# First keys loaded as soon as there is a place, the last weight blocks rounded in place, and two blocks moved out of the first layer

## The chip, the cores and the metric

One core of a Trainium2 chip. The metric is device time in microseconds (us) of one execution. All runs quoted are in the fast state. Line numbers (L871) are those of each kernel's own source, so one statement has several: the first layer's ReLU is L871 before and L874 after the change.

## The reference

An attention block feeds a Fourier mixing block with a two-layer network. Eight batches, 576 rows, 8 heads of 64:

```python
q_s = softmax(q, axis=-1);  k_s = softmax(k, axis=2)      # q, k, v: (8, 8, 576, 64)
kv = np.einsum('bhsd,bhse->bhde', k_s, v)
x = np.einsum('bhsd,bhde->bhse', q_s, kv)                 # then to (8, 576, 512)
mixed = np.real(np.fft.fft(np.fft.fft(x, axis=1), axis=2))
u = x + mixed
un = (u - mean(u)) / np.sqrt(var(u) + 1e-06)
out = u + np.maximum(un @ w_ch1, 0.0) @ w_ch2             # w_ch1: 512x2048, w_ch2: 2048x512
```

(Shortened: the two softmax lines stand for maximum, exp, sum and division; the casts are left out.)

## The kernel before

The rows are worked in groups. The first group runs both layers as plain products while the weights are still being made: 32 blocks of 64-bit words are loaded (16 for each layer), and each is rounded to the form that the products read. Later groups use combined weights made from these, stored and loaded again. While a group's products run on TensorE, the other engines prepare the attention and the spectrum of the next one: the *folds* are sums and differences of rows and columns, most of them on VectorE (tile `eo`), then TensorE multiplies them with the Fourier table, and ScalarE copies that spectrum out of PSUM (tiles `Z` and `ZT`). Tiles of this kernel lie in SBUF, the working memory, or in PSUM, where all its products go; "acc", "ba", "bb" and "bc" are PSUM buffers (banks).

A block is rounded by three engines. ScalarE scales the high half into PSUM (line 343 of the whole text), VectorE shifts and merges it from there (L344, L345), ScalarE scales the low half (L348), and GpSimd adds the two (L349):

```python
def convert(i):
    pair = raws.pop(i).rearrange("p (n w) -> p n w", w=2)
    lo, hi = pair[:, :, 0], pair[:, :, 1]
    # ... out: the block's place in w1sb or w2sb
    n = ("bc", "bb", "bc", "bb")[i] if i < 4 else "acc"
    t = self.ps.tile([P, 512], F32, tag=n, name=n, bufs=3 if i >= 4 else 1)[:]
    to = self.halves()[:, 0:D] if i == NF else out
    ti, V = t.bitcast(I32), nc.vector
    nc.scalar.activation(t, hi.bitcast(F32), ACT.Copy, scale=2.0 ** -112)
    V.tensor_scalar(out=to.bitcast(I32), in0=ti, scalar1=3, scalar2=None, op0=ALU.logical_shift_left)
    V.scalar_tensor_tensor(out=to.bitcast(I32), in0=ti, scalar=-(1 << 31), in1=to.bitcast(I32),
                           op0=ALU.bitwise_and, op1=ALU.bitwise_or)
    nc.scalar.activation(lo, lo.bitcast(U32), ACT.Copy, scale=2.0 ** -29)
    nc.gpsimd.tensor_tensor(out=out.bitcast(I32), in0=to.bitcast(I32), in1=lo, op=ALU.add)
```

Words share places in SBUF. This table says which; the load of block 29 takes the place of block 25, that of block 31 the place of block 26, and each is issued when the sum of the older block is done:

```python
WORDS_AT = [*range(8), 8, 9, 10, *range(3, 8), 0, 1, 2, 8, 9, 10, 4, 5, 6, 7, 8, 11, 12, 7, 13, 8]
```

The first layer ends each of its 16 columns with a ReLU on ScalarE, from one of three PSUM banks; between the columns blocks are rounded, and the rest go between the down products:

```python
for f in range(NF):
    up[f]()          # 4 x 128 rows of products into "ba", "bb" or "bc", then the ReLU on ScalarE
    free(f)
    round_blocks(range(4 + n * f // NF, 4 + n * (f + 1) // NF))      # n = 2 * NF - 14
rest = [lambda i=i: round_blocks([i]) for i in range(4 + n, 2 * NF)]
# ... later, among the down products:
for step in rest[i // 3:i // 3 + 1] if i % 3 == 0 else []:
    step()
```

The keys of a batch's first two blocks, at the end of the folds (`t` is a result of the last fold):

```python
for r in range(2):
    k, v = self.key_places()
    self.nc.vector.tensor_copy(k[0:1, 0:1], t[0:1, 0:1])         # L518, L519: hold the load back
    self.nc.vector.tensor_copy(v[0:1, 0, 0:1], t[0:1, 0:1])
    self.keys_to(b, r, k, v)
```

## Time and profile before

| | before |
|---|---|
| median of 3 runs | 1136.15 us (1133.37 to 1136.38) |
| TensorE busy | 1093.8 of 1135.1 us |
| first group's two layers, first product to the second group's first product | 63.60 to 197.31: 133.7 us |
| the next six groups, to the eighth group's first product | 197.31 to 932.48: 735.17 us |

The two stretches in the last rows are what the change touches, and the document keeps to them. The prediction below reads most of the profile; two more views of the kernel before are needed later. The first is ScalarE's timeline around the first layer's only gap (columns: start us, duration us, engine, line, operation, output and input, count; in brackets the idle time before it and what ended it).

```profile
108.17 0.66 ACT L348 ACTIVATE big<-big 128x512 int32<-128x512 uint32 x1 [6.13 <-DMA big<-in_w_dram]
108.73 0.58 ACT L871 ACTIVATE big<-bb 128x512 f32<-128x512 f32 x1
111.85 0.67 ACT L348 ACTIVATE words<-words 128x512 int32<-128x512 uint32 x1 [2.53 <-DMA words<-in_w_dram]
112.42 0.58 ACT L871 ACTIVATE big<-bc 128x512 f32<-128x512 f32 x1
```

ScalarE's instructions run in the order listed. The low half of block 29 (L348, "big") waits 6.13 us for its words, the ReLU of bank "bb" stands behind it, then the low half of block 31 ("words") waits again, with the next ReLU behind it. So each of the two waits stands before a ReLU, but before a different one, and TensorE has a bank's work in between: it idles 0.98 us.

The second is the queue that issues the loads, SP, with the two loads concerned:

```profile
104.60 0.33 SPq L328 DMA_DIRECT2D big<-in_w_dram  x1
105.84 0.33 SPq L328 DMA_DIRECT2D words<-in_w_dram  x1
```

The words of block 29 are asked for at 104.60 and used from 108.17, 3.57 us later.

### The profile page before, as it was taken

To read this page: it belongs to the slowest core of one execution; us is meant where nothing else is said; L and a number is where in the kernel's file an instruction comes from. 1 tells how busy PE (TensorE), PEld (TensorE's weight loads), DVE (VectorE), ACT (ScalarE), POOL (GpSimd) and SP (SyncE) were. 2 spreads that over 40 slices of the span, in tenths; PEclk is the share of its full clock that TensorE was granted. 3 is DMA by queue.
4 is the path that set the end of the run, shared out by engine and by line. 5 is a ranking of instruction groups with operands and counts; after the bars stand their busy time and mean duration, and the time that the engine had idled before them with its cause. 6 is when DMAs were issued, how large, how long until landed. Compare 5 with 4: busy or idle time off the path is not lost.

```text
span 1135.1 us, 14610 instructions
## 1 busy us (share of the span) xinstructions
PE 1093.8 (96%) x5440; PEld 913.8 (81%) x5440; DVE 543.5 (48%) x1117; ACT 404.0 (36%) x975; POOL 333.7 (29%) x300
## 2 busy tenths in 40 slices
PE   5799989999999999999999999999999999999997
PEld 4644446888888888898889888888889888888886
DVE  6684785477334733484434633583434352203201
ACT  6695614264324423361325232532334152201200
POOL 2065570244022500433023402260034203302320
PEclk9999999999999999999999999999999999999999
DMA  9566686444464344554454535435453344444451
GB/s 308 172 206 212 222 304 201 152 164 167 145 194 161 141 172 145 197 185 151 146 178 150 193 120 196 167 112 183 144 193 149 114 161 152 180 145 155 151 186 55
DMA packets 92582, 193.79 MB, mean 171 GB/s; under 512 B 23121, under 2 KB 59729, under 8 KB 85345
## 3 DMA queue, kind: packets, MB, share of 16 engines
q1 hardware_dynamic: 90712, 191.82, 49.4%
q10 hardware_dynamic: 1800, 1.05, 0.3%
q8 instruction: 43, 0.70, 0.3%
q14 instruction: 27, 0.21, 0.1%
HBM read 168.72 MB, written 28.31 MB: 174 GB/s over the span
## 4 chain that ended last, share of the span: by engine, by line
PE 73%; DVE 10%; DMA 6%; ACT 5%; issue 3%; POOL 2%; SPq 1%; ACTq 0%; POOLq 0%; DVEq 0%
PE bb L939 14%; PE bb L977 12%; PE ba L939 9%; PE bc L939 9%; PE ba L977 7%; PE bc L977 7%; PE acc L560 3%; DMA k<-in_kT_dram 3%; PE acc L642 2%; PE acc L759 2%; DVE eo L681 1%; PE bc L878 1%; PE tr L839 1%; PE tr L546 1%; PE acc L735 1%
## 5 line engine op out<-in xcount | busy, mean ns | idle before, releaser
L939 PE MATMUL bb<-unT,big 128*128 128x256 f32 x768 | 187.4, 381 | 0.8 <-DVE u L911 0.8
L977 PE MATMUL bb<-big 128*128 128x256 f32 x768 | 172.4, 379 | 4.5 <-DVE u L907 4.5
L977 PEld LDWEIGHTS bb<-big 128*128 128x128 f32 x768 | 145.1, 190 | 25.8 <-DVE u L907 5.7
L939 PEld LDWEIGHTS bb<-unT,big 128*128 128x128 f32 x768 | 142.8, 190 | 24.6 <-DVE u L907 2.6
L355 POOL TENSOR_TENSOR big<-big 128x512 f32<-128x512 f32 (+1 forms) x38 | 46.6, 1226 | 307.6 <-ACT big L951 306.8
L939 PE MATMUL bc<-unT,big 128*128 128x256 f32 x512 | 125.3, 379 | 0.0
L951 ACT ACTIVATE big<-big 128x512 f32<-128x512 f32 x96 | 60.3, 629 | 179.0 <-DVE big L950 178.5
L939 PE MATMUL ba<-unT,big 128*128 128x256 f32 x512 | 123.6, 379 | 0.2 <-ACT unT L843 0.2
L977 PE MATMUL bc<-big 128*128 128x256 f32 x512 | 116.0, 379 | 0.5 <-DVE x L994 0.5
L977 PE MATMUL ba<-big 128*128 128x256 f32 x512 | 114.8, 379 | 0.0
L977 PEld LDWEIGHTS bc<-big 128*128 128x128 f32 x512 | 96.1, 190 | 14.3 <-DVE x L994 0.9
L977 PEld LDWEIGHTS ba<-big 128*128 128x128 f32 x512 | 95.7, 190 | 12.1
L939 PEld LDWEIGHTS bc<-unT,big 128*128 128x128 f32 x512 | 95.1, 190 | 12.6
L939 PEld LDWEIGHTS ba<-unT,big 128*128 128x128 f32 x512 | 95.1, 190 | 12.2 <-ACT unT L843 0.5
L911 DVE TENSOR_TENSOR u<-bb,s 128x512 f32<-128x512 f32 x40 | 27.6, 691 | 144.8 <-PE bb L977 88.2
L599 ACT ACTIVATE q<-q,qm 128x64 f32<-128x64 f32 x240 | 62.1, 339 | 25.1 <-DVE qm L597 25.1
L363 POOL TENSOR_TENSOR unT<-unT 128x512 f32<-128x512 f32 x8 | 14.2, 1772 | 188.7 <-DVE unT L362 188.7
L907 DVE TENSOR_TENSOR u<-bb,s 128x512 f32<-128x512 f32 x40 | 27.6, 690 | 72.2 <-PE bb L939 38.7
L989 POOL TENSOR_TENSOR x<-x,u 128x512 f32<-128x512 f32 x14 | 17.7, 1267 | 143.0 <-DVE u L911 74.6
L950 DVE TENSOR_TENSOR big<-bc,u 128x512 f32<-128x512 f32 x64 | 44.1, 689 | 22.8 <-PE bc L939 21.9
L903 ACT COPY s<-ba 128x512 f32<-128x512 f32 x40 | 23.4, 585 | 85.5 <-PE ba L939 46.2
L843 ACT COPY unT<-tr 128x512 f32<-128x512 f32 x36 | 20.7, 586 | 79.4 <-PE tr L839 78.8
(237 smaller groups left out, 1650.0 us busy)
## 6 DMA issues: line engine op xcount, KB each, us to landing
big<-w1s SPq DMA_DIRECT2D x64, 896.0 KB
big<-w2s SPq DMA_DIRECT2D x56, 1024.0 KB
big<-in_w_dram SPq DMA_DIRECT2D x21, 512.0 KB
q<-in_q_dram SPq DMA_DIRECT2D x27, 256.0 KB
k<-in_kT_dram SPq DMA_DIRECT2D x24, 288.0 KB
v<-in_v_dram SPq DMA_DIRECT2D x24, 256.0 KB
words<-in_w_dram SPq DMA_DIRECT2D x8, 512.0 KB
mirror<-x SPq DMA_DIRECT2D x14, 256.0 KB
```

The costliest lines, as they stand in the source:

```text
L355: e1.tensor_tensor(out=to(4), in0=at(2), in1=at(3), op=ALU.add)
L560: nc.tensor.matmul(pk, lhsT=ks[:, c, :], rhs=v[:, c, :], start=(c == 0), stop=(c == NC - 1))
L599: nc.scalar.activation(heads[:, h, :], heads[:, h, :], ACT.Exp, bias=m[:, h:h + 1])
L642: nc.tensor.matmul(px[:, r * P:(r + 1) * P], lhsT=qT[:, r, :], rhs=self.kvr[b % 2][:, r, :], start=True, stop=True)
L759: nc.tensor.matmul(pm[:, at:at + size], lhsT=z(k)[0:rows], rhs=cd[0:rows, at:at + size], start=True, stop=(k != 0))
L903: nc.scalar.copy(temp("s1"), box["ba"][:])
L907: V.tensor_tensor(out=temp("u2"), in0=box["bb"][:], in1=box["s1"][:], op=ALU.add)
L911: V.tensor_tensor(out=temp("u3"), in0=box["bb"][:], in1=box["s1"][:], op=ALU.add)
L939: nc.tensor.matmul(bank()[:, i, :], lhsT=w[:, WA_AT[m], k * P:(k + 1) * P], rhs=unT[:, B_AT[m], k, :], start=first and i == 0 and k == 0, ...
L950: V.tensor_tensor(out=hp(i), in0=bank[:], in1=u[:], op=ALU.add)
L951: nc.scalar.activation(hp(i), hp(i), ACT.Relu)
L977: nc.tensor.matmul(bank()[:, i, :], lhsT=h[p][:, A_AT[m], i * P:(i + 1) * P], rhs=w[:, p, :], start=first and i == 0 and p == 0, stop=p == ...
```

## The change

It touches three places. The keys' loads no longer wait for the folds; only the maxima of the keys do, by a *gate*: a VectorE instruction on one element that reads the last fold's result and rewrites a word of the loaded keys, so that what reads the keys comes after it. In the first group these loads are also held back: `hold` writes one word of each of their places, late in the first layer, and a load has to wait for that (*held places*). Blocks from 20 on no longer take a PSUM buffer: their high half is scaled in place, in SBUF. Two blocks more move from the first layer to the second.

```diff
-        held = {12: [("q", D, 3)] * 3}
+        held = {12: [("q", D, 3)] * 3, 15: [("k", S, 2)] * 2 + [("v", NC * P, 2)] * 2}
...
-            t = self.ps.tile([P, 512], F32, tag=n, name=n, bufs=3 if i >= 4 else 1)[:]
+            if i < 20:
+                t = self.ps.tile([P, 512], F32, tag=n, name=n, bufs=3 if i >= 4 else 1)[:]
+            else:
+                t = hi.bitcast(F32)
...
             k, v = self.key_places()
-            self.nc.vector.tensor_copy(k[0:1, 0:1], t[0:1, 0:1])
-            self.nc.vector.tensor_copy(v[0:1, 0, 0:1], t[0:1, 0:1])
             self.keys_to(b, r, k, v)
+            self.gate(t, k[0:1, 0:1])
...
-            n = 2 * NF - 14
+            n = 2 * NF - 16
+            turn = [2 * i if i < 4 else 3 * i - 4 for i in range(12)]
...
-                for step in rest[i // 3:i // 3 + 1] if i % 3 == 0 else []:
-                    step()
+                if i in turn:
+                    rest[turn.index(i)]()
```

## The prediction

> **What bounds the kernel now.** I read the page first (busy time of each engine), then TensorE's waits, because a gap on the engine that sets the end is the only thing that a change of waits can win back, then the timelines around the largest gaps.
>
> ```profile
> PE 1093.8 (96%) x5440; PEld 913.8 (81%) x5440; DVE 543.5 (48%) x1117; ACT 404.0 (36%) x975; POOL 333.7 (29%) x300
> ```
>
> TensorE is busy 1093.8 of 1135.1 us; all that it idles is 41.3 us. A table of busy time by stretch splits this: 22.1 us fall before 63.6 us (the start, before the first layer), 5.05 us in 63.6 to 197.3 (the first group's two plain layers), 1.43 us in 197.3 to 320 (second group), 6.36 us in 320 to 1031, and 6.3 us after that. The change takes no TensorE work away, so the stretches that it touches hold 5.05 + 1.43 + 6.36 = 12.8 us, or 1.1% of the time. This is the ceiling, and I see no way to a gain over 2% (22.7 us).
>
> TensorE's waits put names to those gaps (us in total, times, longest):
>
> ```profile
> PE acc L560 <- ACT ks L547: 10.6, 10, 3.6
> ...
> PE bb L977 <- DVE u L907: 4.5, 3, 1.9
> PE acc L642 <- DVE big L345: 3.1, 1, 3.1
> ...
> PE bb L869 <- ACT big L871: 1.0, 1, 1.0
> ```
>
> Of the first, 8.8 us lie before 60 us and the other three waits, 0.62 us each, belong to the third key block of a batch, which is not changed. The next three are what the change is about.
>
> **The keys.** The three waits of 4.5 us are at 286, 531 and 777 us, in the second, fourth and sixth group. The last one, on three engines (start, duration, instruction, in brackets the idle time before it and its releaser):
>
> ```profile
> 766.84 0.33 SPq L503 DMA_DIRECT2D k<-in_kT_dram  x1
> 767.27 0.38 SPq L505 DMA_DIRECT2D v<-in_v_dram  x1
> 767.74 0.46 SPq L413 DMA_DIRECT2D big<-w2s  x1
> 768.29 0.38 SPq L503 DMA_DIRECT2D k<-in_kT_dram  x1
> ```
> ```profile
> 766.80 0.13 DVE L518 COPY k<-eo 1x1 f32<-1x1 f32 x1
> ...
> 769.76 0.75 DVE L534 TENSOR_REDUCE km<-k 128x1 f32<-128x576 f32 x1 [2.77 <-DMA k<-in_kT_dram]
> ...
> 776.46 0.75 DVE L534 TENSOR_REDUCE km<-k 128x1 f32<-128x576 f32 x1 [4.66 <-DMA k<-in_kT_dram]
> 777.13 0.68 DVE L907 TENSOR_TENSOR u<-bb,s 128x512 f32<-128x512 f32 x1
> ```
> ```profile
> 777.87 1.99 PE L977 MATMUL bb<-big 128*128 128x256 f32 x8 [1.80 <-DVE u L907]
> ```
>
> The tiny copy at the end of the folds lets the key loads go at 766.8; 0.9 us later a 1 MB weight load follows, and the second key block comes behind it. It lands near 776.4, 8.1 us after its issue. Its maximum stands ahead of L907 on VectorE, L907 must empty the bank "bb", and TensorE waits 1.80 us for that bank.
>
> **The rounding.** In the first group TensorE's largest gap ends at 146.28 us:
>
> ```profile
> 144.73 0.68 DVE L344 TENSOR_SCALAR big<-acc 128x512 int32<-128x512 int32 x1
> 145.44 0.69 DVE L345 SCALAR_TENSOR_TENSOR big<-acc,big 128x512 int32<-128x512 int32 x1
> ```
> ```profile
> 146.28 1.13 PE L642 MATMUL acc<-kvr,qT 128*128 128x128 f32 x8 [3.11 <-DVE big L345]
> ```
>
> A rounded block of the second layer holds one of the three "acc" banks from ScalarE's write until VectorE, busy 9.1 of the 10 us from 140 to 150, has read it twice. The product with the queries needs that bank.
>
> [...] (min/median/max in ns):
>
> ```profile
> L604 DVE TENSOR_TENSOR q<-q,qrec x30: 679/693/1604, 124.0 to 857.0; 128x512 f32<-128x512 f32 x30
> L345 DVE SCALAR_TENSOR_TENSOR big<-acc,big x27: 679/681/693, 67.5 to 153.0; 128x512 int32<-128x512 int32 x27
> ```
>
> Two SBUF inputs take up to 1604 ns beside GpSimd; the rounding with one input in PSUM never more than 693. [...]so L344 may gain by reading SBUF. The nearest measure here is L825 (128x512, SBUF to SBUF, a scaling) at 544 ns against 682 ns for L344.
>
> **Part 1, the keys.** Removed: four 0.13 us copies in each of six batches; added: two gates of about 0.14 us. That is nothing. What counts is when the load goes: its place comes free when the previous batch's last two key blocks have been multiplied (228 to 236 us in the second group, instead of 276), 40 us before the folds end. The DMA share in 230 to 240 us was 0.21, so the 1.2 MB (about 3.5 us at the 350 GB/s seen in the full stretches) have room. The gate then finds its data, both maxima follow the folds at once (1.5 us), L907 starts when its bank is full, and the exps no longer hold ScalarE's copies of the spectrum. Gain: 0.80 + 1.92 + 1.80 = 4.5 us. The third and fifth group have the same 8 us load in the chain that ended last, but TensorE had other work and idled only 0.1 to 0.2 us; little comes from there. I book 4.1.
>
> **Part 2, roundings without PSUM.** ScalarE's 0.64 us stays (the other half, SBUF to SBUF, takes 0.67). Twelve blocks lose their PSUM buffer, and the 3.11 us gap goes. Against it stands VectorE's time. From 120 to 166 us VectorE is the tight engine (9.1, 8.2, 9.1, 8.0 and 8.7 us busy in each 10 us), and five blocks are rounded there. L345 now has two SBUF inputs: at worst +0.6 us each, L344 at best -0.14: some +0.3 on average, 1.5 us for five blocks. TensorE needs the folds at 168.39; the first two are ready at 164.6. Of that slack of 3.8 us, 3.1 are used up if TensorE comes earlier, leaving 0.7. So 1.5 - 0.7 = 0.8 us comes back as a wait: gain 3.1 - 0.8 = 2.3 us. Part 1 is needed for this: in 171.0 to 173.7 ScalarE did the key exps late (0.22 us of wait at 174.29), which would otherwise catch an earlier TensorE. The early keys must also give back what they delay at 120 to 130 us, where DMA share was 0.80: the late words (512 KB each) landed at 128.05 and VectorE took the first only at 131.92, so 3 us of delay is free.
>
> **Part 3, two blocks fewer in the first layer.** Blocks 20 and 21 move behind the first down product. Engine order is not text order here: 27 of the 32 roundings (L344) had run by 103.7 us though blocks 22 to 26 are written in the second layer. So the two blocks hardly move in time. The first layer's one gap (0.98 us at 109.46) comes from a ReLU on ScalarE behind a low half that waited 6.13 us for its words; their load is asked for by block 25, not by 20 or 21. Gain 0.3. The four added copies held to the last ReLU of the layer may cost VectorE a short wait near 123 us; part of that 0.3.
>
> Sum: 4.1 + 2.3 + 0.3 = 6.7 us; 1136.15 - 6.7 = 1129.45, I say 1129.5 us.
>
> **Rivals.** (a) *The wait comes back as a DMA wait.* [...]a key load waiting there for its place (waits on L560 of up to 5.9 us are there already) holds back weight or query loads, and queries were late at 724 us (4.38 us). For: the queries go just after, at 245 us. Against: DMA is 47% busy in these groups and weights are four buffers ahead. It would eat part 1: 1133 to 1136. (b) *VectorE becomes the bound of the first group.* If all five roundings double beside GpSimd (+3.5 us) and the held copies stall it by 2 us, the folds end 5 us later, and TensorE gains nothing or loses 2 us there: 1131.5 to 1134. For: VectorE's load; against: GpSimd idles a quarter of that stretch. (c) *All works, and the new order closes small gaps too:* all of 4.5 + 3.1 + 0.98 + 0.5 (the query wait at 135) + 0.4: 9.5 us, 1126.6. (d) *The start is reordered*, since VectorE's and ScalarE's orders are laid out anew: the 22 us of gaps before 63.6 could move by 2 us either way.
>
> **Range and chances.** From (c) with 2 us luck, 1125, to (a) or (b) at their worse end, 1135.5. The runs before spread by 3 us themselves. Faster by over 2% would need nearly twice the ceiling: 0.01. Slower by over 2% needs a new stall of 23 us, over 3 us in every group: 0.02. Within: 0.97.
>
> **What would show it.** Right: "bb L977 <- DVE u L907" near zero among TensorE's waits; key loads issued at the end of the up products; no DMA wait ahead of the maxima L534; "acc L642 <- DVE big L345" gone; L345 at 0.7 to 1.3 us for twelve blocks; a wait under 1.5 us at the first L735 of the first group; the second group starting near 194 instead of 197.3. Wrong: a DMA wait at the gate, queries or weights waited for, TensorE waiting for the folds by over 3 us in the first group, or a start that ends later than 63.6.

## The result, and the profile after

The changed kernel took 1134.22 us (median of 4 runs, 1133.62 to 1136.19) against 1136.27 us for the kernel before on the same chip. The ratio is 0.9991, 95% interval 0.9971 to 1.0011. Ratios here are the mean time of one kernel's fast runs over that of the other's fast runs of the same rounds, so not quite the ratio of the medians. The predicted gain was 6.7 us. Some 1 to 2 us came, and the interval includes no gain at all.

The stretches show that two large things happened, not none:

| us | before | after | gain |
|---|---|---|---|
| start of the first layer | 63.60 | 63.23 | 0.37 |
| first group's two layers | 133.71 | 141.21 | -7.50 |
| next six groups | 735.17 | 727.20 | 7.97 |
| the rest of the profiled span | 202.6 | 202.8 | -0.1 |

**The six groups** gained more than was booked. This is the busy time of each engine in that stretch (start and end, length, then busy us and instructions of TensorE, its weight loads, VectorE, ScalarE and GpSimd; clock, DMA share and GB/s), before, then after:

```profile
197.31:932.48 735.17, 727.38 (x3871) 642.55 (x3871) 366.29 (x750) 264.80 (x658) 201.94 (x165) 1.00 0.47 160
```
```profile
204.44:931.64 727.20, 725.33 (x3871) 643.16 (x3871) 360.87 (x740) 265.13 (x658) 201.79 (x165) 1.00 0.47 162
```

TensorE's gaps are the length less its busy time: 7.79 us before, 1.87 after, so 5.92 us of the gain are gaps. For the other 2.05 us the same 3871 products count less busy time; I did not look into that. What ended the gaps is on VectorE's timeline of the second group, after the change:

```profile
283.74 1.39 DVE L537 TENSOR_REDUCE km<-k 128x1 f32<-128x576 f32 x2
```

Both maxima run at once, with no wait for data. In the second group the first two key blocks are asked for at 235.68 and 254.04, not at 276.04 and 278.35 as before; the prediction had said 228 to 236 for both.

**The first group** lost it. Three of TensorE's waits after the change (us in total, times, longest):

```profile
PE bb L872 <- ACT big L874: 7.4, 1, 7.4
...
PE tr L613 <- issue: 1.6, 2, 1.1
...
PE acc L738 <- ACT ZT L749: 1.1, 1, 1.1
```

"acc <- DVE big", 3.1 us before, is gone, as predicted, and so is "bb <- DVE u". The first line stands in their place. It is the gap of 0.98 us of before, now 7.41 us, on TensorE's timeline after:

```profile
117.21 5.80 PE L872 MATMUL bb<-unT,big 128*128 128x512 f32 x8 [7.41 <-ACT big L874]
122.84 3.60 PE L872 MATMUL bc<-unT,big 128*128 128x512 f32 x8
```

The eight products after the gap take 5.80 us, the next eight 3.60. The granted clock was 1.00 up to 114.5 us, fell within the gap, was 0.50 from 115.5 to 121.2 us and 1.00 from 122.2 us on. From 117.2 to 123.0 us it was 0.63 on average, against 1.00 in the whole of 100 to 130 us before, where the gap was 0.98 us; 0.50 for about 4.3 of the 5.8 us gives both that 0.63 and the 2.1 us lost (my estimate, from 3.67 us for eight products at 1.00 before). So the long gap cost some 2 us more.

ScalarE's timeline after says why TensorE waited:

```profile
111.53 0.65 ACT L347 ACTIVATE big<-big 128x512 f32<-128x512 f32 x1 [9.82 <-DMA big<-in_w_dram]
112.09 0.66 ACT L352 ACTIVATE big<-big 128x512 int32<-128x512 uint32 x1
115.38 0.65 ACT L347 ACTIVATE words<-words 128x512 f32<-128x512 f32 x1 [2.63 <-DMA words<-in_w_dram]
115.94 0.66 ACT L352 ACTIVATE words<-words 128x512 int32<-128x512 uint32 x1
116.49 0.57 ACT L874 ACTIVATE big<-bb 128x512 f32<-128x512 f32 x1
```

Two things differ from before. Both late blocks, 29 and 31, now stand ahead of the one ReLU of "bb" (**order**). And the words of block 29 came at 111.53 instead of 108.17 (**lateness**). For the second, the SP queue after:

```profile
107.98 0.33 SPq L328 DMA_DIRECT2D big<-in_w_dram  x1
110.04 0.33 SPq L328 DMA_DIRECT2D words<-in_w_dram  x1
```

From issue to use it is 3.55 us, as before (3.57). The load went 3.38 us later, because block 25, whose place it needs, was finished later. GpSimd's sums of blocks 24 and 25, before, then after:

```profile
102.04 2.53 POOL L349 TENSOR_TENSOR big<-big 128x512 int32<-128x512 int32 x2 [1.00 <-ACT big L871]
```
```profile
105.01 2.95 POOL L353 TENSOR_TENSOR big<-big 128x512 int32<-128x512 int32 x2 [1.45 <-DVE big L349]
```

They end at 104.57 before and at 107.96 after. After the change they wait for VectorE, and most of the delay arises there (instances of the shift after the change: min/median/max in ns, first and last start):

```profile
L348 DVE TENSOR_SCALAR big<-acc x15: 678/690/692, 65.9 to 91.2; 128x512 int32<-128x512 int32 x15
L348 DVE TENSOR_SCALAR big<-big x5: 415/1489/1507, 97.0 to 112.3; 128x512 int32<-128x512 int32 x5
L348 DVE TENSOR_SCALAR big<-words x4: 415/968/1509, 94.1 to 116.1; 128x512 int32<-128x512 int32 x4
```

The shift from PSUM took 0.68 to 0.69 us in all 15 of these, also where GpSimd was in an addition (67.66, 71.61 and 83.02: 0.68 each). From SBUF it took 0.41 to 0.43 us alone (0.43 at 112.28 and 116.12, GpSimd idle) but up to 1.51 us (at 105.30, with GpSimd adding from 105.01 to 107.96). The six shifts of blocks 20 to 25 take 6.6 us of VectorE's timeline (pairs at 94.07, 97.04 and 102.35) against 3.95 before: 2.65 us more, next to the 3.39 us that block 25 is late. So the durations show the shift from SBUF faster alone, and slower by up to 1.1 us where GpSimd was in an addition (1.29 us alone); they do not show by what mechanism.

The sum of the first group: the ReLU wait 7.41 - 0.98 = 6.43, the half clock 5.80 - 3.67 = 2.13, the new wait for the spectrum's copies 1.15, and less the PSUM wait, 3.11; that is 6.6 us. Another 1.7 us are eight products at the first layer's start that took 5.37 us at a granted clock of 0.68, and 3.67 before; before, the low clock fell some microseconds earlier (0.50 from 53 to 59 us). Other runs show this either way, so I don't count it to the change. Together 8.3 us, against 7.50 measured. Most of the difference is in TensorE's busy time, which rose by 3.2 us in this stretch and not by 2.1 + 1.7; I did not trace it.

### The profile page after: what moved, and what is told of

It is laid out like the page before. It is cut to its first block, busy times and chain, and to the rows that moved or that the text cites. A ratio compares the mean times of both kernels' runs of the same rounds, so it can differ in the third digit from the quotient of the medians.

```text
span 1134.4 us, 14587 instructions
## 1 busy us (share of the span) xinstructions
PE 1094.5 (96%) x5440; PEld 915.5 (81%) x5440; DVE 542.3 (48%) x1109; ACT 404.3 (36%) x975; POOL 335.3 (30%) x304
## 4 chain that ended last, share of the span: by engine, by line
PE 86%; ACT 4%; DMA 3%; DVE 3%; issue 2%; POOL 1%; ACTq 0%; SPq 0%; POOLq 0%; DVEq 0%
PE bb L942 15%; PE bb L980 15%; PE ba L942 10%; PE bc L980 10%; PE bc L942 10%; PE ba L980 10%; PE acc L563 3%; PE acc L645 2%; PE acc L738 2%; PE acc L741 2%; PE acc L762 2%; PE tr L613 1%; PE tr L842 1%; PE bc L881 1%; PE tr L549 1%
## 5 line engine op out<-in xcount | busy, mean ns | idle before, releaser
L602 ACT ACTIVATE q<-q,qm 128x64 f32<-128x64 f32 x240 | 61.6, 339 | 6.1 <-DVE qm L600 6.0
L953 DVE TENSOR_TENSOR big<-bb,s 128x512 f32<-128x512 f32 x32 | 22.1, 690 | 55.6 <-PE bb L942 55.5
```

Source lines behind the costliest of these rows:

```text
L602: nc.scalar.activation(heads[:, h, :], heads[:, h, :], ACT.Exp, bias=m[:, h:h + 1])
L953: V.tensor_tensor(out=hp(i), in0=bank[:], in1=u[:], op=ALU.add)
```

## The experiments

Times are medians; ratios are to the kernel before, with the 95% interval. My theory ("T" in the expectations) was that the keys gain and the in-place roundings lose it again at the first layer's ReLU. The rivals numbered R there are each described in the expectation that names them.

| run | what it is | us | ratio |
|---|---|---|---|
| e1_keys | the keys alone | 1128.86 | 0.9943 [0.9919, 0.9967] |
| e3_nopsum | in-place roundings alone | 1148.16 | 1.0121 [1.0097, 1.0145] |
| e4_two | two blocks fewer alone | 1135.37 | 1.0003 [0.9992, 1.0015] |
| e2_round | the last two together | 1146.48 | 1.0098 [1.0080, 1.0116] |
| e5_behind | change, blocks 29 and 31 behind the last ReLU | 1134.58 | 0.9994 [0.9979, 1.0009] |
| e6_psum20to26 | change, 20 to 26 in PSUM again | 1127.29 | 0.9931 [0.9916, 0.9946] |
| e12_place20to26 | change, 27 to 31 in PSUM again | 1131.80 | 0.9966 [0.9953, 0.9979] |
| e13_adds_dve | change, sums of 20 to 26 on VectorE | 1127.96 | 0.9915 [0.9886, 0.9944] |
| e7_nogate | keys alone, without the gate | 1132.01 | 0.9972 [0.9956, 0.9988] |
| e8_nohold | keys alone, without the held places | 1128.31 | 0.9934 [0.9915, 0.9952] |
| e9_keys_behind | keys, 29 and 31 behind the last ReLU | 1125.20 | 0.9912 [0.9897, 0.9926] |
| e10_best | e9 with 27 to 31 in place | 1128.08 | 0.9943 [0.9924, 0.9962] |

### The parts alone: e1, e3, e4, e2

e1 has the first and third piece of the diff (held places, keys with the gate) on the kernel before.

> Only the key part of the change (early loads, gate, hold); roundings as before. Theory T (the keys gain, the roundings without PSUM lose it again in the first layer): about 1128 us, 8 us under before; the longest wait of TensorE for a ReLU in the first layer stays near 1.0 us; second group starts near 197 us; groups two to seven last 727 us together instead of 735. Rival R1 (the early key loads crowd the first group's words, and so the loss belongs to the keys): second group starts at 203 us or later and the time is 1133 us or more.

Measured: 1128.86 us, a gain of 0.57%, about 6.5 us. Groups two to seven took 727.80 us, all of the full change's gain; the first layer had no long ReLU wait. The keys are not the loss.

e3 has the in-place piece alone:

```diff
-            t = self.ps.tile([P, 512], F32, tag=n, name=n, bufs=3 if i >= 4 else 1)[:]
+            if i < 20:
+                t = self.ps.tile([P, 512], F32, tag=n, name=n, bufs=3 if i >= 4 else 1)[:]
+            else:
+                t = hi.bitcast(F32)
```

> Only the late roundings without PSUM; blocks of the first layer and keys as before. Theory T: ScalarE's halves of blocks 29 and 31 both stand ahead of a ReLU and wait for their words, so TensorE waits 6 to 8 us for that ReLU and then runs slow for some us; second group starts near 204 us; 1142 to 1144 us. Rival R2 (the loss comes from moving blocks 20 and 21): 1132 to 1135 us, no long wait for a ReLU.

Measured: 1148.16 us, 1.2% slower; worse than expected. The ReLU wait is there with 6.8 us, and a second one with it: 4.7 us for ScalarE's copies of the spectrum at the end of the first group.

e4 has the two pieces with `n` and `turn` alone.

> Only the two blocks fewer in the first layer and the new turn; PSUM and keys as before. Theory T: nothing, 1134 to 1137 us, ReLU wait near 1.0 us, second group starts near 197 us. Rival R2: 1142 us or more.

Measured: 1135.37 us, no difference.

e2 has e3's and e4's pieces together, and the keys as before.

> Both rounding parts (no PSUM from block 20, two blocks fewer), keys as before. If the parts add up: the change's 1134.2 plus the 6 to 8 us that the keys gained, 1140 to 1142 us; ReLU wait of 6 to 8 us; second group starts near 204 us. If the two blocks fewer do nothing beside the in-place rounding either, as they did alone: about 1148 us as with the in-place rounding alone, second group near 209 us.

Measured: 1146.48 us; its second group starts at 207.01. The parts don't add up: e1 gains some 6.5 us and e2 loses some 11, which would make 1140, and the full change took 1134. In e2 the copies of the spectrum are waited for 5.4 us, in the full change 1.1. So the early keys are worth more in company than alone. The likely reason is the one that the prediction gives in its part 2: they take the late exps off ScalarE there. No run tests it apart.

### Order or lateness: e5, e6, e12, e13

e5 removes the order. In the whole change, both blocks are gated behind the last ReLU of the layer:

```diff
             f = i % NF
+            if i in (29, 31):
+                self.gate(self.h0[:, NF - 1, :], pair[0:1, 0:1, :])
             out = (self.w1sb if i < NF else self.w2sb)[:, f, :]
```

> The whole change, and a one-element VectorE gate that holds blocks 29 and 31 behind the last ReLU of the first layer; everything else as in the change. Theory T (the order on ScalarE is the loss): no wait for a ReLU at all, second group starts between 193 and 197 us, 1124 to 1128 us. Rival R3 (the roundings from SBUF cost VectorE and GpSimd so much beside each other that the first group is late anyway): second group starts at 201 us or later, 1131 us or more.

Measured: 1134.58 us, no gain. The wait of 7.4 us for the ReLU is gone, but its time came back as several waits of the second layer and the folds, of which two, in TensorE's waits of e5:

```profile
PE acc L739 <- ACT ZT L750: 3.3, 1, 3.3
PE bc L882 <- POOL s L361: 3.3, 1, 3.3
```

The second is named for GpSimd; the last ReLU before it on ScalarE, at 120.30, stood behind exps of the queries, whose load had been issued at 112.60, after the stores of the late blocks, and landed near 117.3. In e9 that load was issued at 108.40. The issue time is not the whole of it: in e6 the load went at 112.61 too, but its exps began at 115.43. My theory that order alone made the loss fell here, with one reservation: the gate may have a price of its own. e10, below, settles that in part.

e6 gives PSUM back to blocks 20 to 26 only:

```diff
-            if i < 20:
+            if i < 27:
```

> The whole change, but blocks 20 to 26 keep their PSUM buffer and only 27 to 31 are rounded in place. ScalarE's order, read before the run, puts one ReLU behind the high half of block 29 and the next behind block 31, not one behind both. Theory T2 (the loss is the order on ScalarE together with words that come late because VectorE and GpSimd slow each other on blocks 20 to 26 in SBUF): block 29's words are waited for until about 108 us as before, TensorE waits 0.5 to 2 us for a ReLU instead of 7.4, second group starts at 193 to 198 us, 1125 to 1131 us. Rival R4 (any late block in place brings the long wait, whatever blocks 20 to 26 do): wait of 5 us or more, 1133 us or more.

Measured: 1127.29 us. This one condition brings back the whole loss: ReLU wait 0.47 us, second group from 194.44 (the prediction had said 194). On ScalarE's timeline of e6 the ReLU of "bb" stands behind one half of block 29 only (L346, the high half) and ahead of block 31, and the words are there at 106.08, not at 111.53:

```profile
106.08 0.67 ACT L346 ACTIVATE big<-big 128x512 f32<-128x512 f32 x1 [6.66 <-DMA big<-in_w_dram]
106.64 0.57 ACT L873 ACTIVATE big<-bb 128x512 f32<-128x512 f32 x1
107.12 0.68 ACT L351 ACTIVATE big<-big 128x512 int32<-128x512 uint32 x1
```

e12 is the opposite: blocks 20 to 26 in place, 27 to 31 in PSUM (`if i < 20 or i > 26`).

> The counterpart of the run with 20 to 26 in PSUM: the whole change, but only blocks 20 to 26 are rounded in place and 27 to 31 keep PSUM. ScalarE's order, read before the run, has the low halves of blocks 29 and 31 both ahead of one ReLU, as in the change. Theory T2: block 29's words are waited for until about 111 us, TensorE waits 5 to 7 us for the ReLU, second group starts at 201 to 206 us, 1131 to 1137 us. Rival R6 (it is the in-place rounding of 29 and 31 itself): wait under 2 us, second group before 199 us, 1130 us or less.

Measured: 1131.80 us. The ReLU wait is 6.7 us, with eight products at 5.82 us after it, though the blocks ahead of the ReLU, 29 and 31, have their PSUM. Its median is some 2.5 us under the full change's (second group from 199.22), but the intervals of the two ratios overlap, so a cost of blocks 27 to 31 on top of 20 to 26 is not shown. In the profiles, 1.7 of the 5.2 us between the starts of the second group are the low clock at the start of the change's first layer; and e12 has no wait for the spectrum's copies, 1.1 us in the change. The shifts in e12:

```profile
L347 DVE TENSOR_SCALAR big<-big x4: 414/1500/1508, 94.8 to 101.6; 128x512 int32<-128x512 int32 x4
L347 DVE TENSOR_SCALAR big<-words x3: 415/1503/1506, 91.9 to 103.1; 128x512 int32<-128x512 int32 x3
```

e13 takes GpSimd out of the collision: in the whole change the sums of blocks 20 to 26 go to VectorE.

```diff
-            nc.gpsimd.tensor_tensor(out=out.bitcast(I32), in0=to.bitcast(I32), in1=lo, op=ALU.add)
+            adder = nc.vector if 20 <= i < 27 else nc.gpsimd
+            adder.tensor_tensor(out=out.bitcast(I32), in0=to.bitcast(I32), in1=lo, op=ALU.add)
```

> The whole change, except that the last addition of blocks 20 to 26 is done by VectorE instead of GpSimd[...]. Question: why are the late words of blocks 29 and 31 asked for 3.4 and 4.2 us later than before? Theory A (collision): the shift of these blocks out of SBUF takes up to 1.5 us because GpSimd adds at the same time; with no GpSimd addition there every shift of blocks 20 to 26 takes about 0.41 us, though VectorE gets seven additions of some 0.7 to 1.2 us more. The load of block 29 is then asked for some 1 to 3 us earlier than in the change (107.98), TensorE's wait for the ReLU falls from 7.4 to 4 to 6 us, time 1129 to 1133. Theory B (the order alone: without PSUM's pace ScalarE simply has both low halves ahead of the ReLU and the words come when the store queue lets them): shifts may get short, but the load still goes at 107.5 to 109, wait 7 us or more, time 1134 to 1137.

Measured: 1127.96 us, ratio 0.9915 (the kernel before took 1137.97 us on that chip, so the ratio is the better figure), and the result was correct. Every shift from "big" is now short, in e13's instances:

```profile
L347 DVE TENSOR_SCALAR big<-big x5: 414/415/428, 97.6 to 108.3; 128x512 int32<-128x512 int32 x5
L347 DVE TENSOR_SCALAR big<-words x4: 414/421/1503, 93.5 to 111.9; 128x512 int32<-128x512 int32 x4
```

The one long shift, near 94 us, starts at the end of one of GpSimd's sums of earlier blocks; in the change the shift of 1.5 us at 94.07 stands beside the next such sum (93.99 to 95.29). The load of block 29 goes on e13's SP queue 4.08 us earlier than in the change:

```profile
103.90 0.33 SPq L328 DMA_DIRECT2D big<-in_w_dram  x1
105.80 0.33 SPq L328 DMA_DIRECT2D words<-in_w_dram  x1
```

This bears out theory A, the collision, and the effect is larger than expected: the longest ReLU wait is 1.4 us. Two reservations. A sum on VectorE is also shorter, 0.68 us against 1.29 to 1.47 for each on GpSimd, so not all of the 4.08 us need be the collision; the 2.65 us above are the part that the shifts show. And with the sums moved, the order on ScalarE changed too; the ReLU of "bb" now runs at 101.36, ahead of both late blocks. So e13 doesn't separate order from lateness. With order mended and the words still late (e5) nothing was won; with both mended (e6, e13) all of it.

### The gate and the held places: e7, e8

e7 is e1 without the line `self.gate(t, k[0:1, 0:1])`.

> Keys loaded early and held in the first group as in the first experiment, but without the gate that holds their maxima behind the folds. Theory T (what counts is that the loads are early): groups two to seven last 727 to 729 us, 1127 to 1130 us. Rival R5 (the gate is what keeps the maxima and the exps from cutting into the folds): groups two to seven last 731 us or more, 1132 us or more.

Measured: 1132.01 us. The six groups took 732.20 us, between 735.17 (before) and 727.80 (e1), one profile each: the early load without a gate is worth about 3.0 us, and the gate saves another 4.4. In e7 the three waits of 4.5 us that the prediction named are gone too, but in the same three groups (the second, fourth and sixth) TensorE waits 1.70, 0.67 and 2.02 us for something else, 4.4 us in all. Its waits over the whole run, of which these are a part:

```profile
PE tr L608 <- issue: 3.2, 3, 1.7
PE tr L608 <- DVE q L602: 2.7, 2, 2.0
```

The queries' transposes wait for VectorE's division of the queries (L602). So the gate is not only a safeguard against a wait for data; by its place it keeps the key maxima behind the folds, and thereby other work in its turn. Before the change the late loads did that; the gate keeps it, and so is not a gain of its own over the kernel before.

e8 is e1 without the held places in `hold`.

> Keys early and gated, but not held in the first group, so the third batch's first keys are loaded as soon as the queue comes to them. In the trace of the change the held keys were issued only at 166 us, not at 120 to 130 us as predicted, so the hold may bind little. If so: 1127 to 1131 us and the second group starts at 195 to 198 us. If the 1.2 MB come at the start, they crowd the first batch's loads: first layer starts 2 us or more later, 1131 us or more.

Measured: 1128.31 us, the same as e1. The held places did nothing here.

### A version that beats both: e9, e10

e9 is e1 with e5's gate for blocks 29 and 31; PSUM and the split of blocks stay as before.

> Only the key part, roundings in PSUM as before, and the low halves of blocks 29 and 31 held behind the last ReLU of the first layer. Theory T: the ReLU wait of about 1 us goes, but the two blocks then come later to VectorE and hold their PSUM buffers later; second group starts at 195 to 198 us; 1127 to 1131 us, no clear gain over the keys alone. If the order on ScalarE is worth more than its wait, 1125 us or less.

Measured: 1125.20 us (1124.37 to 1126.64), ratio 0.9912, the fastest median of all and better than expected. No ReLU waits in the first layer; of the PSUM wait 1.9 us are left; the second group starts at 193.19. Moving the two late blocks works here, where the words of 29 are asked for at 102.87; in e5 it was 106.47.

e10 is e9 with blocks 27 to 31 in place.

> Keys as changed, blocks 27 to 31 rounded in place, blocks 20 to 26 in PSUM, blocks 29 and 31 held behind the last ReLU, first layer's 18 blocks as before. Theory T2: neither the wait for a ReLU nor the one for the acc bank; second group starts at 192 to 196 us, 1123 to 1127 us. Rival R3 (five in-place roundings beside GpSimd make VectorE late for the folds): waits of 2 us or more for the folds or for ScalarE's copies of the spectrum, second group at 198 us or later, 1129 us or more.

Measured: 1128.08 us. The PSUM wait is gone, but a wait of 3.5 us for the spectrum's copies stands in its place, and the second group starts at 199.48. Its profile also has the low clock at the first layer's start (5.37 us for eight products at 63.00), so part of the 2.9 us over e9 may be that. Having PSUM free was not worth anything there.

e10 also answers e5. Both have the early keys, the gate on 29 and 31, and 27 to 31 in place; in e5 blocks 20 to 26 are in place as well, and two blocks fewer are in the first layer, which did nothing alone (e4). The ratios are 0.9943 and 0.9994, with intervals apart: with the order mended in both, blocks 20 to 26 in place cost some 6 us. But e5's wait for the spectrum's copies need not come from those blocks, since e10 has it too:

```profile
PE acc L739 <- ACT ZT L750: 3.5, 1, 3.5
```

## Why the prediction was wrong

The time lies in the range; the size did not hold: 6.7 us predicted, some 1 to 2 measured, and by the interval not even the direction is certain. That the time still lies in the range is partly luck: a gain of 8 us in the six groups and a loss of 7.5 us in the first group, neither of them the size predicted, nearly cancel.

- **Ceiling and bound**: right. The stretch sums were the right tool, and the gains of e6 and e9, 0.7 to 0.9%, stay within the 12.8 us.
- **Part 1, the keys**: mechanism right, size too small. Booked 4.1 us; the six groups gained 7.97. Of the named waits, 4.5 us went, all of them. Beyond them, 1.4 us of smaller waits went (0.8 of it a wait of the up products for VectorE, L911, in the sixth group) and 2.05 us of busy time, which stays unexplained. In the second group the first key block went when predicted, the second at 254.04; the first keys of all went at 165.8 us, not at 120 to 130, and the harm feared there did not come.
- **Part 2, the failed step**: "some +0.3 on average, 1.5 us for five blocks". The PSUM wait vanished as said, 3.11 us, and a wait for the spectrum's copies of 1.15 us came back, near the 0.8 foreseen. But twelve blocks lose their PSUM, and only five got a cost; blocks 20 to 26, rounded while the first layer runs, got none. They are the loss: with them alone in PSUM again (e6) the ratio is 0.9931 instead of 0.9991, some 7 us. The instruction was wrong too. The prediction feared L345, with two SBUF inputs; its twin hardly moved (ten of twelve at 0.68 to 0.69 us, the other two at 1.21 and 1.66, both beside an instruction of GpSimd). The shift, for which I had booked a gain of 0.14 us, took up to 0.8 us more. The prediction had measured a slowdown beside GpSimd itself (L604, up to 1604 ns), took a gain for L344 from L825 (my estimate, from its 544 ns), and did not join the two. Alone (e3) the part that was to gain 2.3 us lost some 13, though the prediction did say that it needs the early keys.
- **Part 3, where it came out**: "their load is asked for by block 25, not by 20 or 21. Gain 0.3." Moving two blocks did nothing alone (e4). But the loads of 29 and 31 do wait for blocks 25 and 26, and those are among the twelve that part 2 changes. I followed that chain to block 25 and did not ask what part 2 does to block 25. It finished 3.4 us later, and with ScalarE's new order the gap of 0.98 us became 7.41, with 2.1 us of half clock after it.
- **Rivals**: (b) was the nearest, doubled roundings on VectorE, and its mark of 1131.5 to 1134 just misses the median; but it put the end at the folds. The path was the words' load and ScalarE's order. (a) did not happen in the six groups: their gaps fell to 1.87 us. (d), a reordered start: 0.4 us.

That blocks 20 to 26 in place make the loss is shown by e6, and against e10 also with the order mended. That GpSimd's sums slow their shifts is shown by the durations in e13 (the five from "big" took 0.41 to 0.43 us there, a median of 1.49 in the change). What stays open: how the 7.4 us divide between order and lateness, since e5, e6 and e13 each moved more than one thing; how much of e13's gain is only its shorter sum; and why 27 to 31 in place bring the wait for the spectrum's copies in e10.

## What to carry to other kernels

A buffer that an operation waits for also paces the engines around it. Before taking it away, list every instance that loses it, not only the ones at the wait, and follow what each one's end releases: here a load, then ScalarE's next instructions, then TensorE. When an operand moves from PSUM to SBUF, look at whether GpSimd works beside it: here the shift went from 0.69 us to 0.41 alone, and to 1.5 beside GpSimd's additions. And try the parts of a change alone: here one part was worth more than the whole.
